# q and k of batches 1 to 7 turned by DMA transposes from SBUF to SBUF instead of on TensorE

## Chip, cores and metric

The kernel runs on one core of one Trainium2 chip. The metric is the device time of one execution in microseconds (us), lower is better. Inputs and output are float32 in HBM; the kernel computes in bf16 with float32 accumulation in PSUM.

## What is computed

A forgetting attention (causal, with a decay from the cumulated log of f) feeds a SwiGLU feed-forward network. B = 8 batches, H = 8 heads, S = 576 tokens, D = 64; the network is 512 wide with 1536 inner columns, over 4608 tokens.

```python
scores = scale * np.matmul(q, k.transpose(0, 1, 3, 2))
log_f = np.log(np.clip(f, 0.0001, 1.0))
cum = np.cumsum(log_f, axis=-1)
decay = cum[:, :, :, None] - cum[:, :, None, :]
scores = np.where(causal, -1000000000.0, scores + decay)
attn = softmax(scores)                       # over the last axis
attn_out = np.matmul(attn, v)
x = attn_out.transpose(0, 2, 1, 3).reshape(B * S, H * D)
xn = x / sqrt(mean(x * x) + 1e-06) * rms_g
out = (silu(xn @ w_gate) * (xn @ w_val)) @ w_out
```

## The kernel before

The kernel works in two streams that are woven together: the attention of the eight batches, and the feed-forward network over nine groups of 512 tokens. The 576 tokens of a batch are five blocks of 128 (the last one half full), and the heads are taken in four pairs p, as two heads of 64 columns fill 128 partitions.

One batch of attention is this list of work, in this order:

- `load_qk(b)` (line 77) brings q and k of a batch, cast to bf16, into `qb` and `kb` (two buffers each, taken in turn), tokens on partitions, one DMA per block of 128 tokens and tensor, ten per batch. They are issued by POOL, whose issue instructions stand in its own in-order queue, and a ring of eight completion semaphores makes each wait for the one eight before it. `load_v(b)` (line 87) brings v with five DMAs on SP's queue; SP also issues the stores of the results (line 316).
- `transposes(b, p)` (lines 163 to 169) turns q and k of one head pair so that the head columns lie on partitions: five TensorE turns against an identity matrix into one PSUM bank `tr`, then one DVE copy to `QT` or `KT`. So 40 turns and 8 copies per batch. The pool of `tr` has one buffer.
- `scores4` and `scale_v` (lines 158 to 182): the last key block against the last query block, and v scaled with the decay, `Vs`, on POOL.
- `scores(b, p, bank)` (lines 202 to 213): score matmuls of a pair into PSUM, exponentials on ACT into `PT`, the causal zeros put in by POOL selects.
- `values(b, h)` (lines 231 to 235): attention weights times `Vs` into one PSUM buffer `po`, and division by the row sums on DVE into x.
- `norm(b)` (lines 245 to 252): squares on ACT, then `ms` and `rs` on POOL (two small instructions), then the scaling into `xn` on DVE.
- `transpose_x(b, dc)` (lines 258 to 265): x turned on TensorE, again through the bank `tr`, into `xT`.

The network's work is `gate` (lines 296 to 306: 4 + 4 matmuls of 512 columns, a tanh on ACT, two DVE operations; twelve per group) and `project` (lines 311 to 316: twelve matmuls, a copy on ACT, a store; four per group).

Batch 0's attention is written out first. Then a loop over the network's work writes ahead of each piece as much of the attention of batches 1 to 7 as a running sum of costs asks for; the first number of each entry in `attention` is that cost. `load_qk(b + 1)` stands ahead of the attention of batch b. The tile framework takes this written order, reorders it within each engine by its own scheduling, and places the semaphores; the built order of each engine's instructions can be read from the program. All engines run their own queue in order.

Of the kernel before, what the change touches and what calls it, by code (L numbers as in the profile page):

```python
# [9 lines left out]
BF16 = mybir.dt.bfloat16  # L10
# [13 lines left out]
def kernel(  # L24
# [12 lines left out]
    nc = tc.nc  # L37
# [3 lines left out]
    NB = 5  # L41
# [11 lines left out]
    qkt = ctx.enter_context(tc.tile_pool(name="qkt", bufs=2))  # L53
# [13 lines left out]
    qb = [ldp.tile([128, NB, H * D], BF16, name=f"qb{i}") for i in range(2)]  # L67
    kb = [ldp.tile([128, NB, H * D], BF16, name=f"kb{i}") for i in range(2)]
# [83 lines left out]
    QT, KT, PT = {}, {}, {}  # L152
    xs, xTs = {}, {}

    def scale_v(b):
        for j in range(NB):
            v32 = v32s.pop((b, j))
            n = min(128, S - j * 128)
            dj = decT[0:n, j, b * H:(b + 1) * H]
            nc.gpsimd.tensor_tensor(Vs[b % 2][0:n, j, :, 0:D], v32[0:n, :, :], bcast(dj, D), ALU.mult)  # L160
            nc.gpsimd.tensor_copy(Vs[b % 2][0:n, j, :, D], dj)

    def transposes(b, p):
        for src, store, nm in ((qb[b % 2], QT, "QT"), (kb[b % 2], KT, "KT")):
            tp = ps_tr.tile([128, NB * 128], BF16, name="tr")
            for j in range(NB):
                nc.tensor.transpose(tp[:, j * 128:(j + 1) * 128], src[:, j, p * 128:(p + 1) * 128], ident)  # L167
            t = store[b, p] = qkt.tile([128, NB * 128], BF16, name=f"{nm}{p}")
            nc.vector.tensor_copy(t, tp)

    def scores4(b):

        for par in range(2):
            sc = ps_sc.tile([128, 512], F32, name="sc")
            rows = slice(par * 64, par * 64 + 64)
            for p in range(4):
                nc.tensor.matmul(sc[:, p * 64:(p + 1) * 64], lhsT=KT[b, p][rows, 512:640],
                                 rhs=QT[b, p][rows, 512:576], start=True, stop=True)
            t = PT4[b % 2][par]
            nc.scalar.activation(t[:, 0:256], sc[:, 0:256], ACT.Exp, scale=scale)  # L180
            d = t[:, 0:256].rearrange("p (h q) -> p h q", q=64)
            nc.gpsimd.affine_select(out=d, in_=d, pattern=[[0, 4], [1, 64]], compare_op=ALU.is_ge,
                                    fill=0.0, base=0, channel_multiplier=-1)
# [10 lines left out]
    def scores(b, p, bank):  # L194
        for par in range(2):
            h = 2 * p + par
            if bank == 0:
                PT[b, h] = ptp.tile([128, 1536], BF16, name="PT")
            rows = slice(par * 64, par * 64 + 64)
            sc = ps_sc.tile([128, 512], F32, name="sc")  # L200
            for kj, q0, n, c in BANKS[bank]:
                nc.tensor.matmul(sc[:, c:c + n], lhsT=KT[b, p][rows, kj * 128:(kj + 1) * 128],  # L202
                                 rhs=QT[b, p][rows, q0:q0 + n], start=True, stop=True)
            t = PT[b, h]
            nc.scalar.activation(t[:, bank * 512:(bank + 1) * 512], sc, ACT.Exp, scale=scale)  # L205
            if bank == 0:
                d = t[:, 0:128]
                nc.gpsimd.affine_select(out=d, in_=d, pattern=[[1, 128]], compare_op=ALU.is_ge,  # L208
                                        fill=0.0, base=0, channel_multiplier=-1)
            if bank == 2:  # L210
                d = t[:, 512:1408]
                d = bass.AP(tensor=d.tensor, offset=d.offset, ap=[d.ap[0], [384, 3], [1, 128]])
                nc.gpsimd.affine_select(out=d, in_=d, pattern=[[0, 3], [1, 128]], compare_op=ALU.is_ge,  # L213
                                        fill=0.0, base=0, channel_multiplier=-1)
# [10 lines left out]
    def values(b, h):  # L225
        if h == 0:
            xs[b] = xp.tile([128, NB, DM], F32, name="x")
        po = ps_o.tile([128, NB, D + 1], F32, name="po")
        for qi in range(NB):
            for kj in range(qi + 1):  # L230
                nc.tensor.matmul(po[:, qi, :], lhsT=weights_of(b, h, qi, kj), rhs=Vs[b % 2][:, kj, h, :],  # L231
                                 start=(kj == 0), stop=(kj == qi))
        r = small.tile([128, NB], F32, name="rden")
        nc.vector.reciprocal(r, po[:, :, D])  # L234
        nc.vector.tensor_tensor(xs[b][:, :, h * D:(h + 1) * D], po[:, :, 0:D], bcast(r[:, :], D), ALU.mult)  # L235
        PT.pop((b, h))
# [3 lines left out]
    def norm(b):  # L240
        x = xs.pop(b)
        sq = small.tile([128, NB], F32, name="sq")
        junk = xnp.tile([128, DM], BF16, name="junk")
        for j in range(NB):
            nc.scalar.activation(junk, x[:, j, :], ACT.Square, accum_out=sq[:, j:j + 1])  # L245
        ms = small.tile([128, NB], F32, name="ms")
        nc.gpsimd.tensor_scalar(ms, in0=sq, scalar1=1.0 / DM, op0=ALU.mult, scalar2=1e-6, op1=ALU.add)
        rs = small.tile([128, NB], F32, name="rs")
        nc.gpsimd.tensor_tensor(rs, ms, mhalf, ALU.pow)  # L249
        xn = xns[b] = xnp.tile([128, NB, DM], BF16, name="xn")  # L250
        for j in range(NB):
            nc.vector.tensor_scalar_mul(xn[:, j, :], x[:, j, :], rs[:, j:j + 1])  # L252

    def transpose_x(b, dc):
        xn = xns[b]
        tp = ps_tr.tile([128, NB * 128], BF16, name="tr")
        for j in range(NB):
            nc.tensor.transpose(tp[:, j * 128:(j + 1) * 128], xn[:, j, dc * 128:(dc + 1) * 128], ident)  # L258
        t0 = b * S
        while t0 < (b + 1) * S:  # L260
            g = t0 // GT
            t1 = min((g + 1) * GT, (b + 1) * S)
            if g not in xTs:
                xTs[g] = xtp.tile([128, NDC, GT], BF16, name="xT")
            nc.vector.tensor_scalar_mul(xTs[g][:, dc, t0 - g * GT:t1 - g * GT],  # L265
                                        tp[:, t0 - b * S:t1 - b * S], rg[:, dc:dc + 1])
            t0 = t1

    def attention(b):

        a = []
        for p in range(4):
            a.append((0.6, lambda p=p: transposes(b, p)))
        a.append((0.2, lambda: (scores4(b), scale_v(b))))
        for p in range(4):
            for bank in range(3):
                a.append((0.35, lambda p=p, bank=bank: scores(b, p, bank)))
                if p > 0 and bank > 0:
                    a.append((0.45, lambda h=2 * (p - 1) + bank - 1: values(b, h)))
        a.append((0.45, lambda: values(b, 6)))  # L280
        a.append((0.45, lambda: values(b, 7)))
        a.append((0.0, lambda: norm(b)))
        for dc in range(NDC):
            a.append((0.3, lambda dc=dc: transpose_x(b, dc)))
        return a
# [45 lines left out]
    for _, work in attention(0):  # L331
        work()
    stream = []
    for b in range(1, B):
        stream.append((0.0, lambda b=b: (load_qk(b + 1), load_v(b + 1)) if b + 1 < B else None))
        stream += attention(b)
# [43 lines left out]
```

## Time and profile before

| | |
|---|---|
| device time, median of 2 runs | 487.24 us (486.93 to 487.54) |
| span of the profiled execution, first to last instruction | 484.0 us |
| time around the span | 3.2 us |
| PE matmul busy | 423.9 us, 88% of the span |
| DVE, ACT, POOL busy | 54%, 46%, 39% |
| granted TensorE clock | 1.000 |
| DMA queue of POOL's loads / of SP's DMAs | 36.6% / 14.9% of 16 engines' span |

The profile has one row per group of instructions with line, engine, operation, tiles (written <- read), count and mean time, and behind it the idle time of the engine before them with what ended most of it. In a timeline a row is: start, duration, engine, line, operation, tiles, count, and in brackets the idle time ahead with its releaser. A window row has the busy time of each engine between two moments. PE is TensorE, DVE VectorE, ACT ScalarE, POOL GpSimd, SP the queue of SyncE, which only issues DMAs here. Matmuls are pipelined, so their durations overlap; what one costs on the engine is the distance to the next one's start.

### The profile page before, as it was taken

The numbers are of one execution on the slowest core, as the hardware profiler recorded it, in microseconds if no ns is written. First come the engines' busy times: TensorE is split into PE (matmuls) and PEld (weight loads), VectorE is DVE, ScalarE is ACT, GpSimd is POOL, SyncE is SP. The second block draws the span as 40 slices with busy tenths as digits, with TensorE's granted clock in tenths as the row PEclk, the third lists the DMA queues.
The fourth block names the chain that finished last, engine by engine and source line by source line (L and its number), as shares of the span: only waits on it lengthen the run. The fifth ranks groups of instructions, "written<-read, shape, count | busy, mean of one in ns | idle before, by whom it ended". The sixth has DMA issues, their size and how long they took to land.

```text
span 484.0 us, 8505 instructions
## 1 busy us (share of the span) xinstructions
PE 423.9 (88%) x3317; PEld 207.6 (43%) x3317; DVE 260.3 (54%) x534; ACT 222.1 (46%) x436; POOL 187.7 (39%) x335
## 2 busy tenths in 40 slices
PE   0491707999999999999999999999999999999996
PEld 0231403454544454445444544454444544444442
DVE  3210326478447844784478457745774577373670
ACT  3060321664465437544754474447444744232321
POOL 8539990665182518252825282513111211000000
PEclk9999999999999999999999999999999999999999
DMA  9999991594190419041903290010001000201102
GB/s 151 175 195 178 191 187 33 36 65 99 65 120 3 100 66 119 3 100 67 120 1 77 70 118 0 1 66 23 3 0 66 23 1 0 88 1 45 43 1 87
DMA packets 123080, 33.73 MB, mean 70 GB/s; under 512 B 113760, under 2 KB 118368, under 8 KB 123040
## 3 DMA queue, kind: packets, MB, share of 16 engines
q0 software_dynamic: 79744, 14.16, 36.6%
q1 hardware_dynamic: 43296, 19.03, 14.9%
q8 instruction: 26, 0.43, 0.4%
q14 instruction: 14, 0.11, 0.1%
HBM read 37.90 MB, written 9.44 MB: 98 GB/s over the span
## 4 chain that ended last, share of the span: by engine, by line
PE 67%; POOL 13%; issue 6%; DMA 6%; ACT 5%; DVE 2%; POOLq 0%; ACTq 0%
PE ff L311 20%; PE ff L296 14%; PE ff L304 13%; PE sc L202 7%; PE po L231 5%; PE tr L167 4%; DMA wv<-in_moe_w_val_dram 3%; PE tr L258 3%; POOL Vs_104 L160 2%; DMA qb_100<-in_q_dram 2%; ACT junk L245 2%; POOL Vs_105 L160 2%; POOL rs L249 2%; ACT PT L205 2%; POOL qb_100 L77 2%
## 5 line engine op out<-in xcount | busy, mean ns | idle before, releaser
L205 ACT ACTIVATE PT<-sc 128x512 bf16<-128x512 f32 x192 | 105.1, 599 | 87.6 <-PE sc L202 73.8
L296 PE MATMUL ff<-xT,wg 128*128 128x512 bf16 x432 | 114.7, 382 | 0.7 <-DVE xT L265 0.6
L304 PE MATMUL ff<-xT,wv 128*128 128x512 bf16 x432 | 114.0, 380 | 0.0
L311 PE MATMUL ff<-wo,hT 128*128 128x512 bf16 x432 | 112.5, 380 | 0.0
L301 DVE SCALAR_TENSOR_TENSOR ga<-th,ff 128x512 f32<-128x512 f32 x108 | 74.2, 687 | 66.9 <-ACT th L299 66.3
L299 ACT ACTIVATE th<-ff 128x512 f32<-128x512 f32 x108 | 64.5, 598 | 82.6 <-PE ff L296 80.9
L306 DVE SCALAR_TENSOR_TENSOR hT<-ga,ff 128x512 bf16<-128x512 f32 x108 | 74.2, 687 | 9.0 <-PE ff L304 0.3
L304 PEld LDWEIGHTS <-wv 128*128 128x128 bf16 x432 | 42.2, 98 | 50.2 <-issue 2.5
L208 POOL TENSOR_SCALAR_AFFINE_SELECT PT<-PT 128x128 bf16<-128x128 bf16 x64 | 19.1, 299 | 97.8 <-ACT PT L205 97.6
L296 PEld LDWEIGHTS <-wg 128*128 128x128 bf16 x432 | 38.6, 98 | 42.0 <-issue 5.6
L314 ACT COPY ores<-ff 128x512 f32<-128x512 f32 x36 | 21.1, 586 | 75.2 <-PE ff L311 74.4
L213 POOL TENSOR_SCALAR_AFFINE_SELECT PT<-PT 128x384 bf16<-128x384 bf16 x64 | 33.0, 528 | 53.2 <-ACT PT L205 53.1
L311 PEld LDWEIGHTS <-hT 128*128 128x128 bf16 x432 | 36.5, 98 | 36.4 <-issue 9.5
L231 PEld LDWEIGHTS <-PT 128*128 128x128 bf16 x896 | 35.7, 102 | 31.2 <-POOL PT L208 9.7
L234 DVE RECIPROCAL rden<-po 128x5 f32<-128x5 f32 x64 | 12.2, 191 | 55.3 <-PE po L231 55.3
L258 PE MATMUL tr<-ident,xn 128*128 128x128 bf16 x160 | 20.6, 229 | 18.3 <-DVE xn L252 18.0
L231 PE MATMUL po<-Vs_104,PT 128*128 128x65 bf16 x448 | 22.7, 206 | 13.6 <-POOL PT L208 9.2
L235 DVE TENSOR_TENSOR x<-po,rden 128x320 f32<-128x320 f32 x64 | 31.4, 490 | 1.7
L245 ACT ACTIVATE junk<-x 128x512 bf16<-128x512 f32 x40 | 25.0, 624 | 9.0 <-DVE x L235 8.4
L258 PEld LDWEIGHTS <-xn 128*128 128x128 bf16 x160 | 12.4, 100 | 37.0 <-DVE xn L252 29.1
L265 DVE TENSOR_SCALAR xT<-tr,rg 128x512 bf16<-128x512 bf16 (+7 forms) x64 | 20.5, 362 | 12.3 <-PE tr L258 12.1
L252 DVE TENSOR_SCALAR xn<-x,rs 128x512 bf16<-128x512 f32 x40 | 18.1, 520 | 13.2 <-POOL rs L249 13.2
(300 smaller groups left out, 387.8 us busy)
## 6 DMA issues: line engine op xcount, KB each, us to landing
out_dram<-ores SPq DMA_DIRECT2D x36, 256.0 KB, 2.0
qb_100<-in_q_dram POOLq DMA_DIRECT2D x16, 128.0 KB, 5.3
kb_102<-in_k_dram POOLq DMA_DIRECT2D x16, 128.0 KB, 5.4
qb_101<-in_q_dram POOLq DMA_DIRECT2D x16, 128.0 KB, 4.4
kb_103<-in_k_dram POOLq DMA_DIRECT2D x16, 128.0 KB, 4.5
wg<-in_moe_w_gate_dram POOLq DMA_DIRECT2D x3, 512.0 KB, 12.7
wv<-in_moe_w_val_dram POOLq DMA_DIRECT2D x3, 512.0 KB, 14.0
wo<-in_moe_w_out_dram POOLq DMA_DIRECT2D x2, 768.0 KB, 12.3
```

Of the source, the lines that this page charges most:

```text
L202: nc.tensor.matmul(sc[:, c:c + n], lhsT=KT[b, p][rows, kj * 128:(kj + 1) * 128], rhs=QT[b, p][rows, q0:q0 + n], start=True, stop=True)
L205: nc.scalar.activation(t[:, bank * 512:(bank + 1) * 512], sc, ACT.Exp, scale=scale)
L213: nc.gpsimd.affine_select(out=d, in_=d, pattern=[[0, 3], [1, 128]], compare_op=ALU.is_ge, fill=0.0, base=0, channel_multiplier=-1)
L231: nc.tensor.matmul(po[:, qi, :], lhsT=weights_of(b, h, qi, kj), rhs=Vs[b % 2][:, kj, h, :], start=(kj == 0), stop=(kj == qi))
L245: nc.scalar.activation(junk, x[:, j, :], ACT.Square, accum_out=sq[:, j:j + 1])
L258: nc.tensor.transpose(tp[:, j * 128:(j + 1) * 128], xn[:, j, dc * 128:(dc + 1) * 128], ident)
L296: nc.tensor.matmul(pg, lhsT=wg[:, dc, fc * 128:(fc + 1) * 128], rhs=xT[:, dc, :], start=(dc == 0), stop=(dc == NDC - 1))
L299: nc.scalar.activation(t, pg, ACT.Tanh, scale=0.5)
L301: nc.vector.scalar_tensor_tensor(a, in0=t, scalar=1.0, in1=pg, op0=ALU.add, op1=ALU.mult)
L304: nc.tensor.matmul(pv, lhsT=wv[:, dc, fc * 128:(fc + 1) * 128], rhs=xT[:, dc, :], start=(dc == 0), stop=(dc == NDC - 1))
L306: nc.vector.scalar_tensor_tensor(hTs[g][:, fc, :], in0=a, scalar=0.5, in1=pv, op0=ALU.mult, op1=ALU.mult)
L311: nc.tensor.matmul(po, lhsT=hTs[g][:, fc, j * 128:(j + 1) * 128], rhs=wo[:, fc, :], start=(fc == 0), stop=(fc == NFC - 1))
```

## The change

For batches 1 to 7 `transposes` is no longer called. A new `turn(b)` issues ten DMA transposes on SP's queue, one for each block of 128 tokens of q and of k. Each reads [128 tokens, 512 columns] of `qb` or `kb` in SBUF and writes, for each of the four head pairs, [128 columns, 128 tokens] into one tile `QTd` or `KTd` that holds all four pairs (two buffers each). In the list of a batch's work it has a cost of 0.0 and stands at the head, so the running sum that weaves the two streams has 2.4 less per batch. Batch 0 is turned as before, but into the new, larger tiles.

```diff
+    first = {}
+
+    def turn(b):
+        for src, store, nm in ((qb[b % 2], QT, "QTd"), (kb[b % 2], KT, "KTd")):
+            t = qkt.tile([128, 4, NB * 128], BF16, name=nm)
+            for j in range(NB):
+                nc.sync.dma_start_transpose(out=t[:, :, j * 128:(j + 1) * 128], in_=src[:, j, :])
+            for p in range(4):
+                store[b, p] = t[:, p, :]
+
     def transposes(b, p):
         for src, store, nm in ((qb[b % 2], QT, "QT"), (kb[b % 2], KT, "KT")):
             tp = ps_tr.tile([128, NB * 128], BF16, name="tr")
             for j in range(NB):
                 nc.tensor.transpose(tp[:, j * 128:(j + 1) * 128], src[:, j, p * 128:(p + 1) * 128], ident)
-            t = store[b, p] = qkt.tile([128, NB * 128], BF16, name=f"{nm}{p}")
+            if p == 0:
+                first[nm] = qkt.tile([128, 4, NB * 128], BF16, name=f"{nm}d")
+            t = store[b, p] = first[nm][:, p, :]
             nc.vector.tensor_copy(t, tp)
 ...
     def attention(b):
 
         a = []
-        for p in range(4):
-            a.append((0.6, lambda p=p: transposes(b, p)))
+        if b > 0:
+            a.append((0.0, lambda: turn(b)))
+        else:
+            for p in range(4):
+                a.append((0.6, lambda p=p: transposes(b, p)))
         a.append((0.2, lambda: (scores4(b), scale_v(b))))
```

## The prediction, made before the changed kernel ran

> **What bounds the kernel now.** I read the page first (busy shares, then the chain that ended last), then the windows by stage, then PE's timeline for its idle gaps.
>
> ```profile
> span 484.0 us, 8505 instructions
> PE 423.9 (88%) x3317; PEld 207.6 (43%) x3317; DVE 260.3 (54%) x534; ACT 222.1 (46%) x436; POOL 187.7 (39%) x335
> PE 67%; POOL 13%; issue 6%; DMA 6%; ACT 5%; DVE 2%; POOLq 0%; ACTq 0%
> ```
> ```profile
> 60.00:81.00 21.00, 7.79 (x54) 4.15 (x52) 7.58 (x17) 3.61 (x10) 13.33 (x23) 1.00 0.77 131
> 81.00:100.00 19.00, 17.63 (x186) 8.95 (x184) 9.92 (x22) 13.07 (x25) 10.66 (x20) 1.00 0.58 38
> 124.00:172.00 48.00, 46.43 (x394) 22.99 (x394) 28.86 (x59) 25.91 (x52) 22.63 (x40) 1.00 0.55 70
> ```
>
> The window columns are length, then busy time of PE, weight loads, DVE, ACT, POOL, then granted clock, DMA share and GB/s. From 124 us on one batch takes 48 us and PE is busy 46.4 of them: PE sets the pace there. Up to 81 us it does not: PE works 7.8 of 21 us while POOL works 13.3. Of the span, 484.0 us, the timed runs show 487.24, so 3.2 us lie around it.
>
> ```profile
> 72.66 0.29 PE L258 MATMUL tr<-ident,xn 128*128 128x128 bf16 x1 [10.45 <-DVE xn L252]
> ...
> 117.47 0.23 PE L258 MATMUL tr<-ident,xn 128*128 128x128 bf16 x1 [0.96 <-DVE xn L252]
> ...
> 166.18 0.23 PE L258 MATMUL tr<-ident,xn 128*128 128x128 bf16 x1 [0.96 <-DVE xn L252]
> ```
>
> These are the first x turns of batches 0, 1 and 2. PE idles there because xn is late, and xn waits for `rs`, a small POOL instruction in norm. POOL executes in order, so whatever stands ahead of `rs` in POOL's queue sets this gap. That is the wait that I follow below.
>
> **What is removed.** Per batch 40 PE turns and 8 DVE copies go, for batches 1 to 7.
>
> ```profile
> 124.11 0.44 PE L167 MATMUL tr<-ident,qb_100 128*128 128x128 bf16 x5
> 124.39 0.81 PE L311 MATMUL ff<-wo,hT 128*128 128x512 bf16 x3
> ...
> 128.45 0.44 PE L167 MATMUL tr<-ident,qb_100 128*128 128x128 bf16 x5
> 128.83 0.20 PE L177 MATMUL sc<-QT_1280,KT_1288 64*128 64x64 bf16 x2
> ```
> ```profile
> L169 DVE COPY QT_666<-tr x1: 491/491/491, 81.4 to 81.4; 128x640 bf16<-128x640 bf16 x1
> ```
>
> Matmuls overlap, so the price of five turns is the pitch to the next instruction: 0.28 us before a projection, 0.38 us before scores. Eight groups make 2.2 to 3.0 us a batch; I take 2.5, since part of the 0.10 more is the change to scores, which stays. For batches 2 to 7 that is 15 us. Batch 1's turns lie in the start-up, costed below. The copies (8 x 0.49 = 3.9 us of DVE's 28.9 in 48) are worth nothing themselves: PE's 46.4 us cover them.
>
> The skill prices this otherwise. The Trainium skill, "TensorE: Matmul & The Clock Gate", Part 4, gives a PE turn about 275 ns in a kernel's context; by it the 240 turns of batches 2 to 7 would be 66 us, an estimate. The trace's pitch (0.06 us a turn) decides.
>
> **What is added: 70 DMAs of 128 KB on SP's queue.** The trace has none; nearest rows, SP's issue times first, then median landing times:
>
> ```profile
> 41.46 0.37 SPq L87 DMA_DIRECT2D v_202<-in_v_dram  x1
> ...
> 43.73 5.29 SPq L87 DMA_DIRECT2D v_206<-in_v_dram  x1
> ...
> 53.06 0.58 SPq L87 DMA_DIRECT2D v_650<-in_v_dram  x1
> ```
> ```profile
> out_dram<-ores SPq DMA_DIRECT2D x36, 256.0 KB, 2.0
> qb_100<-in_q_dram POOLq DMA_DIRECT2D x16, 128.0 KB, 5.3
> ...
> qb_101<-in_q_dram POOLq DMA_DIRECT2D x1, 128.0 KB, 16.0
> kb_103<-in_k_dram POOLq DMA_DIRECT2D x1, 64.0 KB, 5.8
> ```
>
> Below: 0.37 us of SP for one transpose, as a load on free queues. Above: 5.3 us, what a 128 KB load in 256-byte pieces needs to land, and what one SP issue took against full queues. The nearest row is the same queue in the same stretch: from 41.46 to 53.06 SP got away 896 KB of v, or 1.66 us per 128 KB. I take 2.0 us, as a transpose scatters into smaller pieces.
>
> The skill disagrees with itself. The Trainium skill, "VectorE: DVE Perf Modes", "The three transpose paths", gives a 128x128 block 1309 ns by DMA against 390 ns on TensorE, and advises TensorE where PSUM will do; four blocks in a row would be 5.2 us. "Advanced Engine Details and Errata", "X-Bar Transpose (TRN2)", states 350 to 400 GB/s, an estimated 0.35 us. No run here shows either yet.
>
> **What moves.** In the built order the change does more than drop instructions. `transposes` and `transpose_x` shared the one `tr` bank, so batch 1's turns stood behind batch 0's x turns. Now batch 1's scores stand before those, and all of batch 1's attention before the bulk of the first gates. POOL's queue changes with it: the loads of batches 3 and 4 now stand ahead of batch 1's `rs`, those of batch 5 ahead of batch 2's last start-up selects. Each load into `qb`/`kb` waits for the transposes that read it.
>
> ```profile
> 20.02 0.89 POOL L77 DMA_DIRECT2D qb_101<-in_q_dram  x1
> ...
> 37.13 0.68 POOL L77 DMA_DIRECT2D kb_103<-in_k_dram  x1
> ...
> 46.07 0.54 POOL L208 TENSOR_SCALAR_AFFINE_SELECT PT<-PT 128x128 bf16<-128x128 bf16 x2
> 46.58 0.99 POOL L213 TENSOR_SCALAR_AFFINE_SELECT PT<-PT 128x384 bf16<-128x384 bf16 x2
> ...
> 52.48 0.89 POOL L77 DMA_DIRECT2D qb_100<-in_q_dram  x1
> ...
> 59.65 0.73 POOL L77 DMA_DIRECT2D kb_102<-in_k_dram  x1
> 60.36 1.09 POOL L160 TENSOR_TENSOR Vs_105<-v_200,decT 128x512 bf16<-128x512 f32 x1
> ...
> 66.04 1.04 POOL L160 TENSOR_TENSOR Vs_104<-v_650,decT 128x512 bf16<-128x512 f32 x1
> ...
> 69.81 0.20 POOL L247 TENSOR_SCALAR ms<-sq 128x5 f32<-128x5 f32 x1
> 70.09 1.21 POOL L249 TENSOR_TENSOR rs<-ms,mhalf 128x5 f32<-128x5 f32 x1
> ...
> 84.50 0.29 POOL L208 TENSOR_SCALAR_AFFINE_SELECT PT<-PT 128x128 bf16<-128x128 bf16 x1 [11.00 <-ACT PT L205]
> ...
> 93.89 0.43 POOL L182 TENSOR_SCALAR_AFFINE_SELECT PT_10_108<-PT_10_108 128x256 bf16<-128x256 bf16 x1
> ```
>
> Start-up, step by step. Batch 1's first q block lands at 20.0 + 16.0 = 36.0 us, its last k block at 37.1 + 5.8 = 42.9. Ten transposes at 2.0 us run from 36 to 56 and land by 59. Behind them on SP stand v_202 to v_208, which now go out at 56 to 60 instead of 41 to 53. POOL keeps its order up to 60.36. From there to batch 1's `rs` it now has: selects of PT4 (0.7), Vs of batch 1 (5.7, from 60.36 to 66.04), 16 selects (8 x 0.25 + 8 x 0.48 = 5.8), batch 3's loads (8 x 0.89 + 2 x 0.7 = 8.5), norm of batch 0 (1.5), Vs and PT4 of batch 2 (6.4), batch 4's loads (8.5), two selects (0.5), most of batch 3's Vs (4.4), norm of batch 1 (1.5): 43.5 us, so 103.9. Two waits come on top: v_208 late (2) and ACT behind in exponentials and squares (3), which makes 109; with 0.5 us for xn, batch 1's x turns start at 109.4. PE itself would be there at about 95, so it idles some 14 us: the old 10.45 us gap is moved to batch 1, not removed.
>
> ```profile
> 469.88 10.38 PE ff L311 x48
> ```
>
> What is left then: the old kernel needed 484.0 - 117.5 = 366.5 us from this point. Less 15 for turns; plus 40 gate matmuls that now stand behind this point (40 x 0.216 from the row above = 8.6); less 1.0 for scores of batch 2 done before. And the norm gaps change:
>
> ```profile
> 157.97 1.05 POOL L160 TENSOR_TENSOR Vs_104<-v_1940,decT 128x512 bf16<-128x512 f32 x1 [3.20 <-PE po L231]
> ...
> 164.40 1.20 POOL L249 TENSOR_TENSOR rs<-ms,mhalf 128x5 f32<-128x5 f32 x1
> ```
>
> The old chain from the last values of a batch to xn is 8.1 us, and PE has about 7 us of gates to cover it. For batch 2 three loads and two PT4 selects now stand inside it (3.0 us more, with 6.4 us of cover: gap 4.7), for batch 3 three loads (2.2 more: gap 3.3). Against 0.96 each that adds 6.1. Sum: 109.4 + 366.5 - 15 + 8.6 - 1.0 + 6.1 = 474.6 us of span, with 3.2 us 477.8; I say 479, as lanes of the load queue shared with transposes can only add.
>
> From batch 3 on the transposes are covered: they wait only for finished stores, for loads a batch old and for the buffer of two batches ago, and stand 45 us of PE work ahead of their scores. Without that cover ten would cost 20 us a batch.
>
> **Rivals.** (a) *POOL never waits and loads fit in gaps*: `rs` at 103.9, norm gaps stay 0.96. Then 104.4 + 359.1 = 463.5, with 3.2 us 467. For it: POOL idles 11.00 us before its select at 84.50, so it had spare time; against: that spare time is what the earlier scores already use.
>
> (b) *The transposes are slow.* SP becomes the bound. A batch on SP is ten transposes at P, five v loads and four stores (about 3.9 us at 0.37 to 0.58 each). It outlasts a 45.5 us batch from P = 4.2; already from 3.8 batch 1 is 18 us late and the total passes 497. At 4.6: 36 + 7 x 49.9 = 385 until batch 7 is turned, then what the old kernel had left:
>
> ```profile
> 367.29 0.20 PE L177 MATMUL sc<-QT_4704,KT_4712 64*128 64x64 bf16 x2
> ```
>
> 480.3 - 367.3 = 113; with 3.7 of tail and 3.2 around, 505; at 5.3, 552. For it: 5.29 us of one SP issue; against: that was against full queues, and 1.66 us per 128 KB held over the same stretch. The skill's 1309 ns per block is this rival's rule.
>
> (c) *No net effect*: later norm gaps eat the whole 2.5 us each (they have the same waiters), 479 + 6 x 1.4 = 487.
>
> **How the numbers follow.** Forecast 0.42 (470 to 488), (a) 0.23, (b) 0.28, (c) 0.07. A measurement of this kernel tells about 2% from no change, that is 477.5 and 497. The forecast's range lies 0.17 under the first, 0.25 inside. Faster: 0.17 + 0.23 = 0.40. Same: 0.25 + 0.06 = 0.31. Slower: 0.28 + 0.01 = 0.29. The range for 8 in 10 reaches down to 464, past (a), and up to 508, past (b) at 4.6 us.
>
> **What would show it.** Right: a batch pitch of 45 to 46 us late in the run; PE idle before batch 1's x turns by 10 to 18 us, released by xn; POOL without its 11 us gap; batch 1's transposes issued between 36 and 60 us. Wrong: SP's issue of a transpose over 3.8 us, PE waiting for KTd or QTd in the steady batches, or PE without a gap between 90 and 110 us.

## The result and the profile after

The kernel after takes **506.73 us** (median of 2 runs, 506.13 to 507.33) against 487.24 us: a ratio of 1.041, 95% interval 1.035 to 1.047. It is slower; the forecast was 479 us. The profiled execution has a span of 505.6 us.

Of the page after: span, PE's busy line, the granted clock in 40 slices and the chain that ended last; then, from the view of DMA issues, the transposes with their count and their median time from issue to landing.

```profile
span 505.6 us, 7980 instructions
...
PE 405.8 (80%) x2988; PEld 196.2 (39%) x3037; DVE 237.2 (47%) x478; ACT 217.6 (43%) x436; POOL 190.1 (38%) x335
...
PEclk9999999997999957998599999999999999999999
...
PE 55%; DMA 17%; POOL 14%; issue 8%; SPq 2%; DVE 2%; ACT 1%; POOLq 0%; ACTq 0%
```
```profile
QTd<-qb SPq DMA_TRANSPOSE x35, 3.5
KTd<-kb SPq DMA_TRANSPOSE x35, 3.8
```

PE's busy time fell by 18 us, from 423.9 us, but its idle time grew from 60 to about 100 us. In the chain PE's share fell from 67% to 55%, and DMA's rose from 6% to 17%. The clock, full in every slice before, dips in slices 10, 15, 16, 19 and 20.

The first x turns of batches 1 to 5 (line 270 of the kernel after) in PE's timeline:

```profile
125.83 0.42 PE L270 MATMUL tr<-ident,xn 128*128 128x128 bf16 x2
...
188.88 0.29 PE L270 MATMUL tr<-ident,xn 128*128 128x128 bf16 x1 [14.28 <-DVE xn L264]
...
247.86 0.29 PE L270 MATMUL tr<-ident,xn 128*128 128x128 bf16 x1 [12.12 <-DVE xn L264]
...
293.94 0.23 PE L270 MATMUL tr<-ident,xn 128*128 128x128 bf16 x1 [0.32 <-DVE xn L264]
...
337.74 0.23 PE L270 MATMUL tr<-ident,xn 128*128 128x128 bf16 x1 [0.32 <-DVE xn L264]
```

Before, batch 1's stood at 117.47 and batch 2's at 166.18. So the kernel after is 8.4 us late at batch 1 and 22.7 us late at batch 2. Batch 3 adds another gap of 12.12 us. From batch 4 on the gap is 0.32 us and a batch takes 43.8 us, less than the 48 before. Three places lose, and the rest wins a part back.

**The two long gaps.** What happens ahead of batch 2's norm, in the timelines of PE, SP and POOL:

```profile
161.09 0.44 PE L214 MATMUL sc<-QTd,KTd 64*128 64x64 bf16 x10
...
167.60 0.63 PE L243 MATMUL po<-Vs,PT 128*128 128x65 bf16 x15
```
```profile
142.16 9.98 SPq L331 DMA_DIRECT2D out_dram<-ores  x4
161.58 6.46 SPq L169 DMA_TRANSPOSE QTd<-qb  x5
168.14 7.59 SPq L169 DMA_TRANSPOSE KTd<-kb  x5
```
```profile
164.45 0.90 POOL L77 DMA_DIRECT2D qb<-in_q_dram  x1 [1.26 <-DMA QTd<-qb]
...
174.44 2.63 POOL L77 DMA_DIRECT2D kb<-in_k_dram  x3 [5.43 <-DMA KTd<-kb]
177.94 1.09 POOL L160 TENSOR_TENSOR Vs<-v,decT 128x512 bf16<-128x512 f32 x1
...
187.08 1.20 POOL L261 TENSOR_TENSOR rs<-ms,mhalf 128x5 f32<-128x5 f32 x1
```

Read them as one chain. SP has been free since 152.1, but batch 4's transposes write the `QTd` and `KTd` buffers that batch 2 reads, and go out only at 161.58, after batch 2's last scores (161.09). They keep SP busy to 175.7. POOL had run ahead with its loads: those of batch 6 overwrite `qb` and `kb` of batch 4 and so wait for just these transposes. Behind seven of these ten loads in POOL's in-order queue stands the `Vs` of batch 4, which could start when batch 2's last values end (168.2) and starts at 177.94; behind it stand the other three loads and batch 2's `rs`, which comes at 187.08. PE, which waits for xn, starts 0.6 us after `rs` ends, idle for 14.28 us. Batch 3 repeats it with the loads of batch 7. From batch 4 on no load is left to issue, and no gap either.

**The start-up.** SP's timeline, then PE's:

```profile
35.45 1.29 SPq L169 DMA_TRANSPOSE QTd<-qb  x1
...
55.90 1.75 SPq L169 DMA_TRANSPOSE KTd<-kb  x1
57.74 10.97 SPq L87 DMA_DIRECT2D v<-in_v_dram  x5
...
83.12 8.70 SPq L87 DMA_DIRECT2D v<-in_v_dram  x5
91.91 4.07 SPq L169 DMA_TRANSPOSE QTd<-qb  x1
96.08 1.21 SPq L169 DMA_TRANSPOSE KTd<-kb  x1
...
115.14 4.77 SPq L169 DMA_TRANSPOSE QTd<-qb  x1
```
```profile
64.38 0.40 PE L189 MATMUL sc<-QTd,KTd 64*128 64x64 bf16 x8 [8.79 <-DMA KTd<-kb]
...
100.74 0.34 PE L189 MATMUL sc<-QTd,KTd 64*128 64x64 bf16 x3 [8.85 <-DMA KTd<-kb]
...
124.18 1.86 PE L319 MATMUL ff<-xT,wv 128*128 128x512 bf16 x4 [7.13 <-DVE ga L316]
```

Batch 1's last transpose leaves SP at 57.65 and its scores start at 64.38, so it took some 6.7 us to land. Batch 2's last two transposes stand behind five v loads that hold SP for 8.7 us. PE waits 8.8 us each time. A third wait, of 7.13 us, stands just ahead of batch 1's x turns: on DVE the gate step `ga` (123.45) stands behind `xn` of batch 1 (122.12), which waits for `rs`.

### The profile page after: what moved, and what is told of

Same layout as the page of the kernel before. It is cut to its first block, busy times and chain, and to the rows that moved or that the text cites. A ratio compares the mean times of both kernels' runs of the same rounds, so it can differ in the third digit from the quotient of the medians.

```text
span 505.6 us, 7980 instructions
## 1 busy us (share of the span) xinstructions
PE 405.8 (80%) x2988; PEld 196.2 (39%) x3037; DVE 237.2 (47%) x478; ACT 217.6 (43%) x436; POOL 190.1 (38%) x335
## 4 chain that ended last, share of the span: by engine, by line
PE 55%; DMA 17%; POOL 14%; issue 8%; SPq 2%; DVE 2%; ACT 1%; POOLq 0%; ACTq 0%
PE ff L326 18%; PE ff L319 13%; PE ff L311 13%; DMA kb<-in_k_dram 6%; PE sc L214 5%; POOL Vs L160 5%; DMA KTd<-kb 5%; PE po L243 4%; DMA v<-in_v_dram 4%; DMA wv<-in_moe_w_val_dram 2%; SPq L169 2%; PE tr L270 2%; POOL kb L77 2%; POOL qb L77 2%; DVE xn L264 2%
## 5 line engine op out<-in xcount | busy, mean ns | idle before, releaser
L326 PE MATMUL ff<-wo,hT 128*128 128x512 bf16 x417 | 96.3, 379 | 1.0 <-issue 0.3
L214 PE MATMUL sc<-QTd,KTd 64*128 64x64 bf16 (+4 forms) x512 | 59.7, 274 | 4.8 <-ACT PT L217 3.1
L326 PEld LDWEIGHTS <-hT 128*128 128x128 bf16 x432 | 40.5, 98 | 46.9 <-issue 2.4
L243 PE MATMUL po<-Vs,PT 128*128 128x65 bf16 x960 | 46.0, 204 | 13.7 <-POOL PT L220 11.5
L243 PEld LDWEIGHTS <-PT 128*128 128x128 bf16 x960 | 40.3, 104 | 33.3 <-POOL PT L220 12.9
L160 POOL TENSOR_TENSOR Vs<-v,decT 128x512 bf16<-128x512 f32 (+1 forms) x40 | 42.0, 1050 | 15.0 <-PE po L243 10.0
L270 PE MATMUL tr<-ident,xn 128*128 128x128 bf16 x160 | 22.0, 241 | 31.3 <-DVE xn L264 31.0
L77 POOL DMA_DIRECT2D kb<-in_k_dram x40 | 34.6, 865 | 18.1 <-DMA KTd<-kb 10.7
L77 POOL DMA_DIRECT2D qb<-in_q_dram x40 | 35.0, 875 | 12.1 <-DMA QTd<-qb 5.8
L264 DVE TENSOR_SCALAR xn<-x,rs 128x512 bf16<-128x512 f32 x40 | 21.6, 597 | 37.9 <-POOL rs L261 37.9
L220 POOL TENSOR_SCALAR_AFFINE_SELECT PT<-PT 128x128 bf16<-128x128 bf16 x64 | 20.1, 320 | 40.8 <-ACT PT L217 40.8
```

The costliest lines, as they stand in the source:

```text
L77: nc.gpsimd.dma_start(out=dst[0:n, j, :].rearrange("p (h d) -> p h d", d=D), in_=src[b, :, p0:p0 + n, :].rearrange("h p d -> p h d"))
L326: nc.tensor.matmul(po, lhsT=hTs[g][:, fc, j * 128:(j + 1) * 128], rhs=wo[:, fc, :], start=(fc == 0), stop=(fc == NFC - 1))
```

## Experiments

Theory A: the loss is a wait, made by loads that run ahead. Loads stand on POOL in front of a norm, and wait for transposes that wait for the scores of two batches before. Theory B: the transposes themselves are dear, by traffic or queue time, wherever the loads stand. A third possibility is that the start-up alone loses. All runs below were timed in three rounds, next to the kernel before (486.4 us in each set).

**e1: three buffers for QTd and KTd.** (Start-up tables share a tile with x in e1 and e5, to make room.)

```diff
-    qkt = ctx.enter_context(tc.tile_pool(name="qkt", bufs=2))
+    qkt = ctx.enter_context(tc.tile_pool(name="qkt", bufs=3))
...
-    fr = consts.tile([BH, S], F32)
+    pre = xp.tile([128, NB, DM], F32, name="x").rearrange("p a b -> p (a b)")
+    fr = pre[0:BH, 0:S]
```

> Three buffers of QTd and KTd instead of two (the early constants fr, cum, dec and ident_f lie in a first buffer of x to make room). Theory A (POOL's in-order queue: loads of q and k that wait for transposes stand ahead of norm's rs): the transposes of a batch wait for the buffer of three batches before, so those of batch 4 go out some 25 us earlier, but those of batch 5 now wait for the last scores of batch 2, and the loads of batch 7 that wait for them stand ahead of batch 2's rs. So the gap ahead of batch 2's x turns stays at 10 to 15 us, the one of batch 3 (12.12 us) falls under 4; about 15 us less with the slow restart, 488 to 495 us. Theory B (the transposes' own time on SP and the DMA engines is what costs): the same 70 transposes, 504 to 509 us, both gaps stay.

Measured 503.70 us (502.55 to 504.66), ratio 1.035 (1.032 to 1.038). The gaps ahead of batches 2 and 3 come as A says (14.10 and 0.32 us), but the time misses A's range, so the trace has to say why. POOL, then PE:

```profile
147.43 1.75 POOL L77 DMA_DIRECT2D kb<-in_k_dram  x2 [14.56 <-DMA KTd<-kb]
```
```profile
149.78 0.90 PE L244 MATMUL po<-Vs,PT 128*128 128x65 bf16 x13 [9.24 <-POOL PT L226]
...
199.48 0.29 PE L271 MATMUL tr<-ident,xn 128*128 128x128 bf16 x1 [14.10 <-DVE xn L265]
```

A third buffer moves the wait by one batch and doesn't remove it. Batch 4's transposes now go out before batch 2's scores end, but late on a busy SP, and batch 6's loads wait 14.56 us for them in front of the selects that PE's values need. Batch 5's transposes take over the wait for batch 2's scores, and batch 7's loads the place ahead of batch 2's `rs`. My expectation counted buffers and not the order on POOL.

**e2: loads held back behind a norm of three batches before.** A tiny POOL copy from `rs` into `qb` and `kb`, which the load then overwrites, keeps the loads of batch b from standing ahead of that `rs`.

```diff
     def load_qk(b):
+        if b - 3 in rss:
+            for t in (qb[b % 2], kb[b % 2]):
+                nc.gpsimd.tensor_copy(t[0:1, :, 0], rss[b - 3][0:1, :])
...
+        rss[b] = rs
         xn = xns[b] = xnp...
```

> Two tiny POOL copies ahead of each batch's loads of q and k, which read the rs of norm three batches before, so that no load can stand ahead of that rs in POOL's queue. The same 70 transposes with the same buffers. Theory A: the gaps ahead of the x turns of batches 2 and 3 (14.28 and 12.12 us) fall under 4 us each, and PE does not restart at half clock there (some 3.5 us each); 474 to 484 us. Theory B: nothing on SP or the DMA engines is less, 502 to 509 us. Theory C (the lower granted clock of TensorE is a state of its own and costs the time): the mean clock stays near 0.96 and the time over 495 us.

Measured 473.63 us (472.54 to 474.11), ratio 0.973 (0.970 to 0.976), just under A's 474. The first x turns of batches 2 and 3:

```profile
167.53 0.23 PE L276 MATMUL tr<-ident,xn 128*128 128x128 bf16 x1 [2.20 <-DVE xn L270]
...
214.78 0.23 PE L276 MATMUL tr<-ident,xn 128*128 128x128 bf16 x1 [0.23 <-DVE xn L270]
```

All 70 transposes are still there; only the loads wait. Both gaps are gone and 33 us come back: A, not B. Against C, the mean clock of the profiled execution is 0.993.

**e3: no turning at all for batches 1 to 7** (their scores read batch 0's turned q and k).

```diff
-            t = qkt.tile([128, 4, NB * 128], BF16, name=nm)
-            for j in range(NB):
-                nc.sync.dma_start_transpose(out=t[:, :, j * 128:(j + 1) * 128], in_=src[:, j, :])
             for p in range(4):
-                store[b, p] = t[:, p, :]
+                store[b, p] = store[0, p]
```

> Leaves out the turning of q and k of batches 1 to 7: their scores are taken from batch 0's turned tiles; loads, scores and all else stay. Says what the change could bring at most if the transposes cost nothing and nobody waited for them. Theory A and B: 464 to 474 us, batch pitch 43 to 45 us, no gap above 4 us after batch 1's x turns. If the change lost its time by the new order of the attention itself and not by the transposes, it stays over 490 us.

Measured 464.00 us (463.70 to 465.18), ratio 0.954 (0.951 to 0.957). Its first x turns of batches 1, 4 and 5:

```profile
116.99 0.29 PE L267 MATMUL tr<-ident,xn 128*128 128x128 bf16 x1 [9.73 <-DVE xn L261]
...
250.46 0.23 PE L267 MATMUL tr<-ident,xn 128*128 128x128 bf16 x1 [0.32 <-DVE xn L261]
...
294.25 0.23 PE L267 MATMUL tr<-ident,xn 128*128 128x128 bf16 x1 [0.32 <-DVE xn L261]
```

From batch 4 to batch 5 it takes 43.79 us, and the kernel after 43.80 (293.94 to 337.74). Where no load is left to wait, the transposes cost PE nothing. One long gap stands here too, 9.73 us ahead of batch 1's x turns: it comes from POOL's new order and needs no transpose.

**e4: batch 1 turned on PE, batches 2 to 7 by DMA, loads held as in e2.**

```diff
-        if b > 0:
+        if b >= 2:
             a.append((0.0, lambda: turn(b)))
```

> Batch 1 is turned on TensorE as before, batches 2 to 7 by DMA, and the loads are held behind rs as in the run with the tiny copies. Theory A with the start-up's share on SP's queue: the start-up is that of the kernel before (x turns of batch 1 near 117 us), every later batch gains about 4 us on 48: 462 to 472 us. Theory B: a transposed batch costs more than a turned one, over 490 us.

Measured 476.24 us (473.56 to 477.56), ratio 0.977 (0.972 to 0.981): no gain over e2, against A. The start-up did get shorter (first project matmul at 117.6 us, 128.8 in e2), but PE waits 22.6 us in all for xn, 14.8 in e2. The longest wait, ahead of batch 0's x turns, is 10.46 us (9.01 in e2); most of the difference lies in gaps of 1.3 to 2.2 us in later batches, like this one:

```profile
260.82 0.23 PE L276 MATMUL tr<-ident,xn 128*128 128x128 bf16 x1 [2.00 <-DVE xn L270]
...
262.93 2.77 PE L332 MATMUL ff<-wo,hT 128*128 128x512 bf16 x6
```

The six matmuls after it take 2.77 us, and six at 274.72 only 1.47 us. Why this order leaves less gate work ahead of the x turns wasn't followed further.

**e5: three buffers for the loads, two for QTd and KTd.**

```diff
-    qb = [ldp.tile([128, NB, H * D], BF16, name=f"qb{i}") for i in range(2)]
+    qb = [ldp.tile([128, NB, H * D], BF16, name=f"qb{i}") for i in range(3)]
...
-            for src, dst in ((q, qb[b % 2]), (k, kb[b % 2])):
+            for src, dst in ((q, qb[b % 3]), (k, kb[b % 3])):
```

> The kernel after, with a third buffer for the loads (qb and kb), two buffers for QTd and KTd as before; first tables of the start-up share a tile of x to make room. POOL's order has seven of batch 7's loads ahead of batch 2's Vs and rs, none ahead of batch 3's. Theory A (norms late because loads ahead of them wait for transposes that wait for the scores of two batches before): batch 6's loads now wait for batch 3's transposes, which are out by about 127 us, batch 7's for batch 4's, which are still out only at about 174. So one long gap instead of two: PE idle of 10 to 15 us before the x turns of batch 2, none over 3 us before those of batch 3, and a time of 489 to 497 us (506.7 less the 9.6 to 13.8 us of the second gap). Rival B (each batch of transposes costs its own traffic or queue time, wherever loads stand): no change, 502 to 509.

Measured 492.13 us (490.64 to 493.58), ratio 1.011 (1.009 to 1.014), in the middle of A's range. Batches 2 and 3 in PE's timeline:

```profile
187.26 0.29 PE L271 MATMUL tr<-ident,xn 128*128 128x128 bf16 x1 [14.23 <-DVE xn L265]
...
234.52 0.23 PE L271 MATMUL tr<-ident,xn 128*128 128x128 bf16 x1 [0.32 <-DVE xn L265]
```

One gap of two is gone, the one whose loads no longer wait, and with it 14.6 us.

**e6: loads held behind the norm of two batches before.** As e2, with `b - 2` for `b - 3`.

> The kernel after, with q and k of batch b loaded only when rs of batch b - 2 is written (a tiny copy from rs into qb and kb ahead of the loads). All loads then stand right behind a norm, never ahead of one. Theory A: no gap over 3 us in the norms of batches 2 to 6, pitch 43.5 to 45 us per batch; the start-up pays, as batch 2's loads begin only after the rs of batch 0 (about 85 us) and its transposes end near 110, so PE waits for KTd of batch 2 by 5 to 15 us: 468 to 482 us in all. Rival B: 500 to 509. Rival C (loads this late starve the steady batches: PE waits for KTd or QTd in each): over 485.

Measured **465.07 us** (463.85 to 466.57), ratio 0.956 (0.953 to 0.959): 3 us below A's range, and faster than both kernels. The start-up price that I expected didn't come. The pitch missed A's 43.5 to 45 us: from batch 1 to batch 4 it is 46.6 us on average ((248.67 - 108.97) / 3), and 43.65 us only from batch 6 to 7, when no load is left. So the hold seems to have a price of its own while loads are issued; which wait makes it stays open. SP, PE and POOL:

```profile
56.06 1.21 SPq L174 DMA_TRANSPOSE KTd<-kb  x1
```
```profile
59.03 0.40 PE L194 MATMUL sc<-QTd,KTd 64*128 64x64 bf16 x8 [3.23 <-DMA KTd<-kb]
...
155.92 0.29 PE L276 MATMUL tr<-ident,xn 128*128 128x128 bf16 x1 [2.21 <-DVE xn L270]
...
248.67 0.23 PE L276 MATMUL tr<-ident,xn 128*128 128x128 bf16 x1 [0.23 <-DVE xn L270]
```
```profile
107.18 1.20 POOL L266 TENSOR_TENSOR rs<-ms,mhalf 128x5 f32<-128x5 f32 x1
...
109.27 1.00 POOL L82 DMA_DIRECT2D qb<-in_q_dram  x1
```

Loads now follow a norm. Batch 1's last transpose leaves SP at 57.27 us, 57.65 in the kernel after, but its scores start at 59.03, 1.8 us later and not 6.7: the loads of batch 2 are not in the DMA queues yet, as POOL issues them from 79.5 us on. No wait for xn is over 2.21 us. Between 85 and 110 us PE's busy time (second number), in the kernel after and in e6:

```profile
85.00:110.00 25.00, 13.71 (x120) 8.07 (x123) 11.17 (x25) 4.37 (x10) 17.05 (x28) 1.00 1.39 148
```
```profile
85.00:110.00 25.00, 23.70 (x166) 11.12 (x164) 18.74 (x35) 12.05 (x27) 14.36 (x27) 1.00 1.14 131
```

So the start-up of the kernel after loses too, and the hold that ends the run-ahead ends that loss.

**e7: e6 with batch 1 turned on PE** (e4's edit on top of e6).

> As the kernel with loads behind the rs of two batches before, and batch 1 turned on PE and DVE as in the kernel before. Theory A: PE's two waits for KTd of batch 1 go (8.9 us), batch 2's wait stays or grows; 464 to 478 us, below the variant with batch 1 by DMA by 2 to 10 us. Rival: the start-up is bound by POOL's own work and not by the transposes, then the two are within 3 us of each other.

Measured 471.43 us (469.90 to 472.15), ratio 0.969 (0.968 to 0.971): the time is in the range, but 6.4 us above e6 and not below it. PE's waits for `KTd` are gone, its waits for xn are 20.1 us, 9.2 in e6; 7.74 of them lie ahead of batch 0's x turns, 1.24 in e6. As in e4, taking batch 1 back to PE trades one wait for another.

**e8: each transpose of batches 6 and 7 issued twice.**

```diff
-            for j in range(NB):
+            for j in [j for j in range(NB) for _ in range(2 if b >= 6 else 1)]:
```

> The kernel after, with each transpose of batches 6 and 7 issued twice (twenty more, about 13 us more of SP's queue in each of these batches). The prediction's step that transposes are covered from batch 3 on, where it is right (late batches, with no loads behind them): no change, within 1.5 us of 506.7. Rival (SP's queue or the traffic of transposes sets the pace of late batches): longer by 8 to 27 us.

Measured 508.46 us (506.61 to 510.04), ratio 1.045 (1.042 to 1.048), which overlaps the interval of the kernel after. It is 1.7 us above 506.73, 0.2 us more than I allowed, and far from the rival's 8. The doubled transposes on SP, and the project matmuls around them:

```profile
280.39 13.63 SPq L169 DMA_TRANSPOSE QTd<-qb  x10
294.07 9.79 SPq L169 DMA_TRANSPOSE KTd<-kb  x7
```
```profile
301.07 0.39 PE L326 MATMUL ff<-wo,hT 128*128 128x512 bf16 x1
...
344.86 0.39 PE L326 MATMUL ff<-wo,hT 128*128 128x512 bf16 x1
```

The pitch is 43.79 us with some 13 us more on SP for each of the two batches. Late in the run the transposes are covered, twice over.

**e9: the kernel before, with e6's hold.**

> The kernel before (PE turns and DVE copies for all batches) with the same hold on the loads: q and k of batch b only after rs of batch b - 2. It shows how much of the 21 us that the held kernel with DMA transposes gains is the hold and how much the transposes. Theory A (the transposes save about 2.5 to 4 us a batch, 18 to 28 us over seven, once no load stands ahead of a norm; before, the loads wait only for PE turns that are done early): the hold alone is worth 0 to 6 us, 480 to 487 us. Rival D (the gain is that of the hold: loads ahead of norms cost the kernel before as well): 466 to 476 us.

Measured 486.12 us (485.05 to 487.67), ratio 1.000 (0.998 to 1.002). The hold alone is worth nothing. So e6's 21 us come from turning by DMA, with the new order of work that this brings, and the loads that run ahead cost the kernel after the 42 us between 506.7 and 465.1.

## Why the prediction was wrong

**The step that failed** is "From batch 3 on the transposes are covered: they wait only for finished stores, for loads a batch old and for the buffer of two batches ago". It names the wait and takes it for free. The buffer of two batches ago comes free only with that batch's last scores (161.09 us for batch 2), just when POOL needs to be through with its loads. The transposes' own results were covered; the loads behind them, and the norm behind the loads, were not. The term of the sum is the norm gaps: predicted 4.7 and 3.3 us, measured 14.28 and 12.12. The three loads that I had counted between `Vs` and `rs` are there. What the sum lacks are the seven ahead of `Vs`, and what they wait for: they make `Vs` of batch 4 start 9.7 us after batch 2's last values (168.2 to 177.94). With the 4.7 us predicted that is 14.4, and 14.28 were measured. e5 and e2 show that it is the wait: take it away for one batch, and one gap goes; hold the loads, and both go.

**The start-up.** The price of a transpose held: ten from 35.45 to 57.65 us, 2.2 us each, 2.0 predicted. What failed is that I followed SP for batch 1 only. Five v loads took 10.97 us there, not 4, batch 2's last two transposes went out at 91.91 and 96.08, and PE waited 8.79 and 8.85 us. Batch 1's x turns were predicted at 109.4 us and came at 125.83. The gap that I had moved to batch 1 is there, but as 7.13 us and not 14, because PE got there only at 117.1 us and not at about 95; e3 has it as 9.73 us. In e6 these turns came at 108.97, near the forecast by coincidence, as POOL's order is another there.

**Left out: slow restarts.** After a long gap PE runs at half speed at first. Window rows after the gap at 188.88:

```profile
188.00:192.00 4.00, 2.90 (x14) 1.14 (x15) 2.72 (x6) 1.20 (x3) 0.97 (x3) 0.50 0.07 4
192.00:196.00 4.00, 4.00 (x20) 1.68 (x20) 2.44 (x6) 1.86 (x4) 1.30 (x3) 0.53 0.00 0
196.00:200.00 4.00, 3.95 (x29) 1.85 (x29) 3.10 (x8) 2.10 (x4) 0.29 (x1) 1.00 0.00 2
```

Some 7 us at a clock of 0.50 are about 3.5 us lost per long gap.

**Right, or nearly.** The turns saved were put at 2.5 us a batch, and late in the run a batch gains 4.2 us (48 to 43.8, where 45 to 46 were forecast), with e3 the same. The 0.28 us for five turns ahead of a projection was too low: in the profile before, two such groups start 1.02 us apart (125.14 and 126.16) with three projection matmuls between them, and at 0.216 us each these leave 0.37 us, so 3.0 us a batch. The smaller norm gap (0.96 to 0.32) gives 0.64 more; some 0.6 us stay open. In the batches after the start-up a transpose costs SP 1.4 us ((6.46 + 7.59) / 10).

**The signs.** Two of the four signs of being right came: batch 1's transposes went out from 35.45 to 57.65 us, and POOL has no gap of 11 us any more (its longest in that stretch is 7.22 us, for ACT). The pitch was shorter than forecast, and so was PE's idle time ahead of batch 1's x turns. Of the signs of being wrong, SP's issue did pass 3.8 us for single transposes in the start-up (4.77 at most); PE never waited for `KTd` or `QTd` in a later batch.

**The rivals.** (b), slow transposes, gives 497 to 505 us, close to what came, but not by its mechanism: it needs 3.8 us a transpose or more, and e8 shows that SP has room for twenty. That 506.7 us falls inside the range for 8 in 10 (464 to 508) is owed to this rival alone, and so luck. (Its time at 5.3 us is 554 and not 552.) (a) fails on its premise, as POOL does wait; that its 467 us is near e6, another kernel, says nothing for it. (c), at 487 us, expects later norm gaps that eat the gain; late in the run they are 0.32 us, shorter than before. Its 1.4 us a batch isn't worked out from any row. A rival that followed a waiting load to what stands behind it was missing; the profile before showed loads waiting on PE's turns without harm, and I took that over.

**Two figures for a transpose.** The Trainium skill, "VectorE: DVE Perf Modes", "The three transpose paths", with 1309 ns for a 128x128 block, spoke against the change. The change did lose, but not by that: four such blocks in one transpose took SP 1.4 us in all and landed in 3.5 to 3.8 us, against the 5.2 us estimated from it. The bandwidth in the Trainium skill, "Advanced Engine Details and Errata", "X-Bar Transpose (TRN2)", an estimated 0.35 us for 128 KB, wasn't reached either (3.5 to 3.8 us to land).

## What to carry to other kernels

When work leaves an engine whose order held other queues back, follow each new wait to the end: what the waiting instruction waits for, when that comes, and what stands behind it in its in-order queue. Loads that may run ahead are not free when their buffer is released late; a load held behind the small instruction that others wait for can be worth more than another buffer. Test a hold on the kernel before as well, so that its gain isn't mixed up with that of the change.

## What the hardware showed that I had not expected

- Half speed after idle time is not told by the gap's length alone. After 14.28 us it lasted about 7 us, after 7.13 us some 3.3 us (124.18 to 127.5). In e4 it set in only 2 us after the end of the gap of 2.00 us, and lasted some 3.3 us (262.9 to 266.2). The Trainium skill, "TensorE: Matmul & The Clock Gate", Part 1, has PE fall to half its clock after an idle window of about 3.4 us and come back after about as much sustained work. The trace agrees in the halving, and in the time to come back for two of these three; the 7 us and the fall after 2.00 us differ.
- The granted clock does not show every stretch at half speed. In the start-up of the kernel after five x turns take 0.74 us, at 90.13 ahead of the gap of 8.85 us and at 101.41 behind it, and only from 103.69 on 0.44 us. The granted clock (third from the end of the window row) reads 1.00 there all the same:

```profile
98.00:104.00 6.00, 3.26 (x28) 2.16 (x29) 0.64 (x2) 0.00 (x0) 0.12 (x1) 1.00 0.91 142
```
```profile
101.41 0.74 PE L270 MATMUL tr<-ident,xn 128*128 128x128 bf16 x5
```

- SP is held by each transpose that it issues: 1.2 us at the least and up to 4.77 us in the start-up, while loads were under way. There a v load held it 2.2 us on average (10.97 / 5).
